# RWKV-7 attention followed by hash-routed experts: first expert's weights loaded during attention, the guard of w cut into 24 pieces among the experts, one outer fallback loop

## The chip, the cores and the metric

The kernel runs on one core of one Trainium2 chip. Time is device time in microseconds (us) of one execution; the median of several executions is given where there are several. A core has five engines with instruction streams of their own: TensorE (PE, with its weight loads as PEld), VectorE (DVE), ScalarE (ACT), GpSimd (POOL) and SyncE (SP, which only issues DMAs here). Each engine works its list in order, and engines wait for each other through semaphores. Transfers are moved by 16 DMA engines, which all queues share.

## The reference

The first part is a linear attention with a state per batch and head (4 batches, 8 heads, 768 steps, head size 40), the second a layer of 8 experts, in which a hash of the token's number chooses the expert.

```python
for t in range(S):
    y[:, :, t] = np.einsum('bhd,bhde->bhe', rt, state)
    Sa = np.einsum('bhde,bhe->bhd', state, at)
    state_decay = state * wt[:, :, None, :] - np.einsum('bhd,bhe->bhde', Sa, bt)
    state = state_decay + np.einsum('bhd,bhe->bhde', vt, kt)
...
expert_idx = token_ids * np.int64(2654435761) % np.int64(E)
for e in range(E):
    xe = x[expert_idx == e]
    out[expert_idx == e] = np.maximum(xe @ w1[e], 0.0) @ w2[e]
```

x is y with the heads side by side: 3072 rows of 320. w1 is 320 by 1024 and w2 1024 by 320 for each expert, all in float32, so each expert has two tensors of 1.31 MB.

## The kernel before

**Attention.** The sequence is cut into 12 chunks of 64 steps. A tile is one chunk of two batches with all heads, 24 tiles in all. The steps of a tile are spread over "ticks": `at_tick(tick, step)` puts a function into a list, which is sorted by tick and then executed once to write the instructions, so the order on each engine is written out by hand, over all tiles. The last tiles stand at ticks 30 and 31. The products of the decays w are formed in six rounds in the tiles `pb` and `qb` (L267 and L268), two buffers of each in the pool `work`. `paced` (L221) makes a DMA wait for the last TensorE instruction written so far, so that a load is not issued long before its tick. Loads of r, v, a, b and k go through SyncE's queue, one to two ticks ahead. Step "y" of a tile (L737) computes its rows of x, `xs`, and stores them with two DMAs from GpSimd's queue to `x_rows` in device memory (L753). At the end of attention its pools are closed, and their memory is used again.

**Routing.** In the ticks from 8 on, small steps sort the tokens: `src_all` and `idx_all` hold the rows of each expert in groups of 128, three groups of an expert and one group for the rests of four experts.

**Experts.** From here the order on an engine is chosen by the tile framework's scheduler, which follows the order of the program, priorities and buffers. `gather` (L938) fetches 128 rows of x with an indirect DMA from GpSimd (`xg`, six buffers), duplicates the last 64 columns on ScalarE, transposes three blocks on TensorE and copies them to `xt` on VectorE. `up` (L949) multiplies with w1 in two halves of four blocks; the blocks are evicted in turn by ScalarE and VectorE into `ht`, and five PSUM banks carry them. `down` (L979) multiplies with w2, and `put` (L969) copies the result on ScalarE and stores it with an indirect DMA. `load_w1` and `load_w2` load an expert's weights from SyncE's queue into two and six buffers; the first loads stand right behind the end of attention (L921, L927, L994).

**The guard and the fallbacks.** The decays are clamped to the range LO to HI for attention. After the experts all of w is read once more in six pieces of 128 by 1280 (L1018 to L1024), on VectorE: clamped, compared with itself, and the differences counted into `wbad`. From the count come four small numbers (L1026 to L1037). If any w was out of range, a slow loop over the sequence computes x anew (L1052), and a second loop (L1098) repeats the experts; the second loop also handles experts with more tokens than there are slots. With these inputs both loops run zero times, but each engine has to load the counts and pass both loops.

Of the kernel before, what the change touches and what calls it, by code (L numbers as in the profile page):

```python
# [8 lines left out]
F32 = mybir.dt.float32  # L9
# [9 lines left out]
def kernel(  # L19
# [18 lines left out]
    P = 128  # L38
# [42 lines left out]
    WP = 6  # L81
    wbad = route.tile([P, WP], F32)


    def load_w1(e, name):
        t = wpool.tile([P, 2 * F + F // 2], F32, tag="w1", name=name)
        nc.sync.dma_start(t[:, 0:2 * F].rearrange("p (c f) -> p c f", c=2), e[0:2 * P].rearrange("(c p) f -> p c f", p=P))
        for x in range(2):
            nc.sync.dma_start(t[x * C:(x + 1) * C, 2 * F:].rearrange("p (f i) -> p f i", i=P),
                              e[2 * P:DM].rearrange("p (f x i) -> p x f i", x=2, i=P)[:, x])  # L90
        return t


    a_ctx = ExitStack()
# [162 lines left out]
    def decays(ri, t_load, t_clamp, t_chain, t_own, t_ex, t_ends, t_pair, t_recip, t_en, t_spread, t_turn):  # L257
# [5 lines left out]
        for i in range(4 * RN):  # L263
            @at_tick(t_load + (0.06 * i if ri > 2 else 0))
            def _(i=i):
                if i == 0:
                    x["pb"] = work.tile([P, HC * D], F32, tag="pb", name="pb")  # L267
                    x["qb"] = work.tile([P, (HC + 1) * D], F32, tag="qb", name="qb")  # L268
# [385 lines left out]
    def tile_b(u, t0):  # L654
# [83 lines left out]
        def _():  # L738
# [12 lines left out]
            for be in range(2):  # L751
                r0 = batch(g, be) * S + n * C
                nc.gpsimd.dma_start(x_rows[r0:r0 + C, :], xs[half(be)])  # L753
# [159 lines left out]

    ET = mybir.EngineType
# [6 lines left out]
    w1s[0] = load_w1(moe_w1[0], "w1_0")  # L921
# [5 lines left out]
    w1s[1] = load_w1(moe_w1[1], "w1_1")  # L927
# [5 lines left out]
    def load_w2(e, name):  # L933
        t = w2pool.tile([P, FP, DM], F32, tag="w2", name=name, bufs=6)
        nc.sync.dma_start(t[:], e.rearrange("(c p) d -> p c d", p=P))
        return t

    def gather(xt, j, idx):  # L938

        xg = mwork.tile([P, DM + C], F32, tag="xg", bufs=6, name="xg")  # L940
        nc.gpsimd.indirect_dma_start(out=xg[:, 0:DM], out_offset=None, in_=x_rows[:],  # L941
# [5 lines left out]
        nc.vector.tensor_copy(xt[:, :, j * P:(j + 1) * P], p[:])  # L947

    def up(xt, w1, ht, n):  # L949
        def part(f):  # L950
            return slice((f % 2) * C, (f % 2 + 1) * C)
        for f0 in range(0, FP, 4):
            banks = []
            for f in range(f0, f0 + 4):
                banks.append(bank([P, n], "up_ps", "up", 5))
                rows = part(f)
                w = 2 * F + (f // 2) * P
                nc.tensor.matmul(banks[-1][:], lhsT=w1[rows, w:w + P], rhs=xt[rows, 2, 0:n], start=True, stop=False)  # L958
            for f in range(f0, f0 + 4):
                p = banks[f - f0]  # L960
                for c in range(2):
                    nc.tensor.matmul(p[:], lhsT=w1[:, c * F + f * P:c * F + (f + 1) * P], rhs=xt[:, c, 0:n],  # L962
# [16 lines left out]
    def down(ht, w2, j, idx, apart):  # L979
        p = bank([P, DM], "dn_ps")  # L980
        for f in range(FP):
            nc.tensor.matmul(p[:], lhsT=ht[:, f, j * P:(j + 1) * P], rhs=w2[:, f, :],  # L982
# [3 lines left out]
    def down_shared(hts, w2q, idx):  # L986
        p = bank([P, DM], "dq_ps")
        for f in range(FP):
            for q in range(4):
                nc.tensor.matmul(p[q * QTR:(q + 1) * QTR, :], lhsT=hts[q][:, f, FULL:SLOTS], rhs=w2q[q][:, f, :],  # L990
# [156 lines left out]
```

## Time and profile before

| | us |
|---|---|
| median of 3 runs | 741.28 (730.99 to 743.15) |
| profiled execution | 735.78 |
| its span, first to last instruction | 734.0 |
| attention, to its last matmul | 450.9 |
| seam: from there to the first `up` matmul | 20.4 |
| experts: from there to the last `down` matmul | 251 |
| from there to the end of the span | 11.5 |

The profile is of one execution. Rows of the timeline give start, duration, engine, line of the kernel, operation, output and inputs, how many of them, and in brackets how long the engine had been idle and what ended that. In the chain of waits a row is start, duration and what the end of the program waited for at that time. "issue" is time in which no wait shows. Windows give for each engine the busy microseconds and the number of instructions, then the clock that was granted to TensorE as a share of full speed, the busy share of the DMA engines and GB/s.

### The profile page before, as it was taken

What the parts mean: (1) busy time and instruction counts of PE and PEld (TensorE: products, weight loads), DVE (VectorE), ACT (ScalarE), POOL (GpSimd) and SP (SyncE); (2) the same over time, 40 slices, a digit from 0 to 9 for tenths busy, and PEclk for the clock granted to TensorE, in tenths of its full rate; (3) what the DMA queues carried; (4) which work ended last, traced back from release to release, by engine and by line L of the source; (5) the groups of instructions that cost most, each with busy time, mean ns of one, the idle gap of its engine ahead of it and who ended that gap; (6) DMA issues with size and microseconds to landing.
All of it is one profiled execution on the core that took longest, in us unless ns stands there. A gap on an engine that the chain in (4) does not pass through costs nothing.

```text
span 734.0 us, 23938 instructions
## 1 busy us (share of the span) xinstructions
PE 613.1 (84%) x10398; PEld 462.2 (63%) x10398; DVE 339.3 (46%) x704; ACT 309.4 (42%) x688; POOL 272.9 (37%) x343
## 2 busy tenths in 40 slices
PE   0436689789978998998998994598999999999993
PEld 0335568668867887887887884254656565565652
DVE  6789968835864684576397212116320110111100
ACT  2475656655775576786855561111110101101110
POOL 1786556443646483465241111503123030210111
PEclk9987679966997698899999998599999999999998
DMA  8565134523463453465244324977413342120000
GB/s 156 112 114 115 23 63 87 117 55 66 95 110 65 74 97 53 84 112 92 39 57 58 71 58 142 351 242 245 145 34 119 115 157 95 44 90 9 27 3 29
DMA packets 156748, 70.15 MB, mean 96 GB/s; under 512 B 134942, under 2 KB 149791, under 8 KB 156640
## 3 DMA queue, kind: packets, MB, share of 16 engines
q1 hardware_dynamic: 146336, 51.53, 31.1%
q0 software_dynamic: 5952, 16.08, 8.8%
q8 instruction: 82, 1.34, 0.7%
q10 hardware_dynamic: 4352, 0.98, 0.7%
q14 instruction: 26, 0.21, 0.1%
HBM read 56.73 MB, written 12.16 MB: 94 GB/s over the span
## 4 chain that ended last, share of the span: by engine, by line
PE 53%; issue 18%; DVE 11%; DMA 6%; POOL 5%; ACT 5%; SPq 1%; POOLq 0%; DVEq 0%; ACTq 0%
PE dn_ps L982 7%; PE up_ps L962 6%; PE r_ps L219 5%; PE y_ps L219 5%; PE s_ps L219 4%; PE rc_ps L219 4%; PE u_ps L219 3%; PE a_ps L219 3%; PE z_ps L529 2%; PE sd_ps L762 2%; POOL xg L941 2%; PE t_ps L534 2%; PE c_ps L219 2%; DMA z_all<-in_k_dram 2%; DVE ub L568 2%
## 5 line engine op out<-in xcount | busy, mean ns | idle before, releaser
L982 PE MATMUL dn_ps<-w,ht 128*128 128x320 f32 x384 | 104.9, 433 | 0.0
L972 POOL DMA_INDIRECT out_dram<-o,idx_all x26 | 25.7, 987 | 190.0 <-ACT o L971 182.8
L962 PE MATMUL up_ps<-xt,w 128*128 128x416 f32 x256 | 93.9, 520 | 0.0
L982 PEld LDWEIGHTS dn_ps<-w,ht 128*128 128x128 f32 x384 | 72.8, 190 | 32.1 <-issue 1.9
L753 POOL DMA_DIRECT2D x_rows<-xs x48 | 26.3, 553 | 149.4 <-DVE xs L750 103.3
L962 PEld LDWEIGHTS up_ps<-xt,w 128*128 128x128 f32 x256 | 47.5, 191 | 45.8 <-issue 45.8
L568 DVE TENSOR_TENSOR ub<-ub,outer 128x31 f32<-128x31 f32 (+15 forms) x186 | 65.0, 349 | 6.4
L565 DVE TENSOR_TENSOR outer<-ub,nb 128x31 f32<-128x31 f32 (+15 forms) x186 | 62.6, 337 | 4.6
L965 DVE TENSOR_SCALAR ht<-up_ps 128x416 f32<-128x416 f32 x32 | 18.9, 591 | 94.8 <-PE up_ps L962 94.8
L947 DVE COPY xt<-xg_ps 128x384 f32<-128x384 f32 x24 | 12.1, 551 | 101.8 <-PE xg_ps L946 101.8
L971 ACT COPY o<-dn_ps 128x320 f32<-128x320 f32 x24 | 10.2, 425 | 101.6 <-PE dn_ps L982 101.6
L703 DVE TENSOR_TENSOR mr<-rc_ps,after 128x1024 f32<-128x1024 f32 x24 | 29.3, 1221 | 50.4 <-PE rc_ps L219 50.4
L529 PE MATMUL z_ps<-ident,z_all 128*128 128x128 f32 x192 | 32.7, 325 | 15.1 <-DVE z_all L460 12.5
L967 ACT ACTIVATE ht<-up_ps 128x416 f32<-128x416 f32 x32 | 15.9, 514 | 63.8 <-PE up_ps L962 63.8
L460 POOL TENSOR_TENSOR z_all<-z_all,qt 128x320 f32<-128x320 f32 x40 | 34.2, 864 | 14.2 <-DMA z_all<-in_k_dram 12.5
L219 PE MATMUL rc_ps<-rt,cv 64*64 64x64 f32 x1536 | 37.5, 243 | 1.9 <-ACT cv L686 1.1
L941 POOL DMA_INDIRECT xg<-x_rows,src_all x26 | 27.2, 1045 | 28.7 <-PE xg_ps L946 15.7
L529 PEld LDWEIGHTS z_ps<-ident,z_all 128*128 128x128 f32 x192 | 26.3, 168 | 17.8 <-DVE z_all L460 12.8
L958 PE MATMUL up_ps<-xt,w 64*128 64x416 f32 x128 | 30.1, 562 | 7.8 <-DVE xt L947 3.2
L351 ACT COPY qt<-qt 64x320 f32<-64x320 f32 (+1 forms) x63 | 31.2, 495 | 12.0 <-DVE qt L326 8.2
L219 PEld LDWEIGHTS rc_ps<-rt,cv 64*64 64x64 f32 x1536 | 30.6, 151 | 8.6 <-issue 5.3
L714 ACT COPY x_all<-nc_ps 64x512 f32<-64x512 f32 x44 | 25.5, 580 | 24.3 <-PE nc_ps L712 23.8
(186 smaller groups left out, 1214.7 us busy)
## 6 DMA issues: line engine op xcount, KB each, us to landing
w<-in_moe_w_dram SPq DMA_DIRECT2D x8, 1280.0 KB, 17.5
w<-in_moe_w_dram SPq DMA_DIRECT2D x8, 1024.0 KB
r<-in_r_dram SPq DMA_DIRECT2D x48, 80.0 KB, 3.3
x_all<-in_v_dram SPq DMA_DIRECT2D x48, 80.0 KB, 3.7
py<-p_rows POOLq DMA_DIRECT2D x24, 160.0 KB
x_rows<-xs POOLq DMA_DIRECT2D x48, 80.0 KB
wt<-in_w_dram SPq DMA_DIRECT2D x6, 640.0 KB, 3.9
z_all<-in_b_dram SPq DMA_DIRECT2D x46, 80.0 KB, 3.3
```

Source lines behind the costliest of these rows:

```text
L219: pe_last[0] = nc.tensor.matmul(out_, lhsT=lhsT, rhs=rhs, start=start, stop=stop, skip_group_check=True).ins
L351: nc.scalar.copy(qt[d[0], d[1], cols], qt[src[0], src[1], cols])
L460: eng.tensor_tensor(t, t, by.rearrange("p (h e) -> p h e", e=D), op=OP.mult)
L529: pe_last[0] = nc.tensor.transpose(dst, src, ident[:]).ins
L565: nc.vector.tensor_tensor(tv, ub[:, 0:j + 1, j:j + 1].to_broadcast([P, j + 1, m]), nb[:, j, j + 1:].unsqueeze(1).to_broadcast([P, j + 1, m ...
L568: nc.vector.tensor_tensor(o, o, tv, op=OP.add)
L703: nc.vector.tensor_tensor(t[:].rearrange("p two h t -> p (two h) t"), p[:].rearrange("p two (h t) -> p (two h) t", t=C), after[:].unsqueez ...
L753: nc.gpsimd.dma_start(x_rows[r0:r0 + C, :], xs[half(be)])
L941: nc.gpsimd.indirect_dma_start(out=xg[:, 0:DM], out_offset=None, in_=x_rows[:], in_offset=bass.IndirectOffsetOnAxis(ap=idx, axis=0))
L958: nc.tensor.matmul(banks[-1][:], lhsT=w1[rows, w:w + P], rhs=xt[rows, 2, 0:n], start=True, stop=False)
L962: nc.tensor.matmul(p[:], lhsT=w1[:, c * F + f * P:c * F + (f + 1) * P], rhs=xt[:, c, 0:n], start=False, stop=(c == 1))
L982: nc.tensor.matmul(p[:], lhsT=ht[:, f, j * P:(j + 1) * P], rhs=w2[:, f, :], start=(f == 0), stop=(f == FP - 1))
```

## The change

- Expert 0's weights are no longer loaded after attention. `first_weights` takes buffers of `pb` and `qb`, which are now in a pool `carry` that stays open, and loads w1 into the two of `pb` and w2 into the two of `qb`, in 12 DMAs at ticks 20.5, 21.1 and so on to 27.1, each paced. `up` and `down` now take a function that gives the slice of a weight.
- The last chunk's stores of x go through SyncE's queue.
- Expert 1's weights are loaded after the first expert's fourth gather has landed (`hold_back`). Gathers have five buffers instead of six, w2 five instead of six.
- The guard is cut into 24 pieces of 128 by 320. `look` issues four loads at the end of each of the experts 0 to 5, `judge` takes four in each of the experts 1 to 6, with four buffers; `verdict` stands ahead of the last expert's `down`s. The scheduler then places them: on SyncE's queue four pieces come first behind attention, a fifth, then the weights of expert 1 (w1, w2), of expert 2, w2 of expert 3, three pieces, w2 of expert 4, four pieces, w2 of expert 5, and the other pieces. On VectorE four pieces and a fifth are judged among expert 0's copies to `xt`, seven ahead of expert 1's copies to `xt`, seven behind these and ahead of expert 1's first eviction, and the last five between its evictions.
- Both fallback loops stand inside one loop that runs once if either is needed, and zero times otherwise; a fourth count tells which.

```diff
-    WP = 6
+    WP = 24
...
+    def hold_back(dma):
+        if held:
+            tc.add_manual_dep(dma.ins, held[-1].name,
+                              mybir.DependencyInfo(mybir.DependencyClass.Sync, mybir.DependencyReason.SCHED_ONLY))
...
-                    x["pb"] = work.tile([P, HC * D], F32, tag="pb", name="pb")
-                    x["qb"] = work.tile([P, (HC + 1) * D], F32, tag="qb", name="qb")
+                    x["pb"] = carry.tile([P, HC * D], F32, tag="pb", name="pb")
+                    x["qb"] = carry.tile([P, (HC + 1) * D], F32, tag="qb", name="qb")
...
-                nc.gpsimd.dma_start(x_rows[r0:r0 + C, :], xs[half(be)])
+                (nc.sync if last else nc.gpsimd).dma_start(x_rows[r0:r0 + C, :], xs[half(be)])
...
+    def first_weights():
+        w1, w2 = moe_w1[0], moe_w2[0]
+        h = HC * D
+        a = [carry.tile([P, h], F32, tag="pb", name=f"w1_0{i}") for i in range(2)]
+        b = [carry.tile([P, (HC + 1) * D], F32, tag="qb", name=f"w2_0{i}") for i in range(2)]
...
+        for i in range(2):
+            for j in range(2):
+                cols = slice(j * F // 2, (j + 1) * F // 2)
+                yield nc.sync.dma_start(a[i][:, cols], w1[i * P:(i + 1) * P, cols])
+            for x in range(2):
+                yield nc.sync.dma_start(a[i][x * C:(x + 1) * C, F:].rearrange("p (f i) -> p f i", i=P),
+                                        w1[2 * P:DM].rearrange("p (f x i) -> p x f i", x=2, i=P)[:, x, 2 * i:2 * i + 2])
+        for i in range(2):
+            for j in range(2):
+                c0 = 4 * i + 2 * j
+                yield nc.sync.dma_start(b[i][:, 2 * j * DM:2 * (j + 1) * DM].rearrange("p (c d) -> p c d", d=DM),
+                                        w2[c0 * P:(c0 + 2) * P].rearrange("(c p) d -> p c d", p=P))
+
+    weights = first_weights()
+    for i in range(12):
+        at_tick(NU - 3.5 + 0.6 * i, order=7)(lambda: paced(next(weights)))
...
+    def look(n):
+        for i in range(len(seen), len(seen) + n):
+            wt = mwork.tile([P, m], F32, tag="wt", name="wt", bufs=n)
+            nc.sync.dma_start(wt[:], wq[:, i * m:(i + 1) * m])
+            seen.append(wt)
+
+    def judge(n):
+        for i in range(len(seen) - n, len(seen)):
+            wt = seen[i]
+            wc = mwork.tile([P, m], F32, tag="wc", name="wc", bufs=1)
+            nc.vector.tensor_scalar(wc[:], wt[:], LO, HI, op0=OP.max, op1=OP.min)
+            nc.vector.scalar_tensor_tensor(wt[:], wc[:], 0.0, wt[:], op0=OP.add, op1=OP.not_equal, accum_out=wbad[:, i:i + 1])
...
+        nc.vector.tensor_scalar(ctl[:, 3:4], ovin[0:1, E - 1:E], 0.0, None, op0=OP.is_gt)
+        nc.vector.tensor_tensor(ctl[:, 3:4], ctl[:, 3:4], bad[:], op=OP.max)
...
+        if e == 0:
+            held.append(g)
+            w1s[1] = load_w1(moe_w1[1], "w1_1")
+            w2s[1] = load_w2(moe_w2[1], "w2_1")
+            held.pop()
...
         if q == 3:
+            if e == E - 1:
+                bad, ctl = verdict()
             down_shared([hts[e - 3 + i] for i in range(4)], [w2s[e - 3 + i] for i in range(4)],
                         idx_all[:, NMT + e // 4:NMT + e // 4 + 1])
+        if 0 < e < E - 1:
+            judge(per)
         for j in range(TPE):
             down(ht, w2s[e], j, idx_all[:, e * TPE + j:e * TPE + j + 1], True)
...
+            look(per)
...
+    some = nc.values_load(ctl_i[0:1, 3:4], min_val=0, max_val=1)
+    with tc.For_i(0, some, 1):
+        nblk = nc.values_load(ctl_i[0:1, 0:1], min_val=0, max_val=S // STEP)
+        with tc.For_i(0, nblk, 1) as i:
```

## The prediction

> **What bounds the kernel now.** I read the page first: busy shares, then the 40 slices.
>
> ```profile
> PE 613.1 (84%) x10398; PEld 462.2 (63%) x10398; DVE 339.3 (46%) x704; ACT 309.4 (42%) x688; POOL 272.9 (37%) x343
> PE   0436689789978998998998994598999999999993
> PEclk9987679966997698899999998599999999999998
> GB/s 156 112 114 115 23 63 87 117 55 66 95 110 65 74 97 53 84 112 92 39 57 58 71 58 142 351 242 245 145 34 119 115 157 95 44 90 9 27 3 29
> ```
>
> TensorE has the work; a slice is 18.35 us. Behind the start-up it is full except at slices 24 and 25 (440 to 477 us), the seam between attention and experts, where the DMA engines suddenly move 351 GB/s, and in the last slice. So the edits are worth what these places and the guard of w cost. Next, the chain of waits in order of time over the seam (start, us, what):
>
> ```profile
> 450.95 0.50 DVE xs L750
> 451.73 0.53 POOL x_rows L753
> 452.26 5.53 DMA x_rows<-xs
> 457.79 0.02 issue
> ...
> 459.63 1.01 POOL xg L941
> 460.65 0.30 issue
> 460.95 0.97 POOL xg L941
> ```
>
> The last rows of x leave at 451.7, land at 457.79 (5.5 us after issue), GpSimd works off its semaphores for 1.84 us, and only then starts the gathers, 1.26 us apart. The timeline of the same stretch gives the end of the seam, and later the first two `up`s:
>
> ```profile
> 469.51 0.87 PE L946 MATMUL xg_ps<-ident,xg 128*128 128x128 f32 x3 [0.37 <-DMA xg<-x_rows,src_all]
> 471.30 3.15 PE L958 MATMUL up_ps<-xt,w 64*128 64x416 f32 x8 [0.91 <-DVE xt L1005]
> ...
> 503.53 1.49 DVE L1024 SCALAR_TENSOR_TENSOR wt<-wc,wt 128x1280 f32<-128x1280 f32 x1
> 503.94 2.08 POOL L941 DMA_INDIRECT xg<-x_rows,src_all  x1 [0.30 <-issue]
> ...
> 511.84 0.24 ACT L943 COPY xg<-xg 128x64 f32<-128x64 f32 x1 [2.19 <-DMA xg<-x_rows,src_all]
> 511.99 0.92 ACT L967 ACTIVATE ht<-up_ps 128x416 f32<-128x416 f32 x2
> 512.56 1.66 PE L958 MATMUL up_ps<-xt,w 64*128 64x416 f32 x6 [1.56 <-ACT ht L967]
> ```
>
> From the last matmul of attention (ends 450.93) to the first of expert 0's `up` are 20.4 us. Expert 1's `up` takes 17.19 us (502.65 to 519.84); in the chain, expert 6's takes 14.83 (660.48 to 675.31): 2.36 lost. ScalarE is in order, and its evictions stood behind copies of gathers that came late. The last view is the tail, by windows of 2 us:
>
> ```profile
> 723.29 0.97 POOL L972 DMA_INDIRECT out_dram<-o,idx_all  x1 [3.34 <-DVE it L1095]
> 724.00:726.00 2.00, 0.00 (x0) 0.00 (x0) 0.00 (x0) 0.00 (x0) 0.26 (x1) 1.00 0.28 94
> 726.00:728.00 2.00, 0.00 (x0) 0.00 (x0) 0.00 (x0) 0.00 (x0) 0.00 (x0) 0.86 0.00 0
> ```
>
> The result has landed by 726; the other 8.0 us of the span (734.0) hold no work, only two loops passed over and the end.
>
> **The change, part by part. (1) Seam.** Expert 0's 2.6 MB are loaded during attention, expert 1's wait behind the fourth gather, the last two pairs of x stores move from GpSimd's to SyncE's queue. Step by step, with the times of before:
> - xs is ready at 451.45. Two stores on SP: the nearest row is `p_rows<-pt`, an SP store of twice the size: 0.48 us on the queue, 2.1/3.0/5.3 us to landing (min, median, max). The second lands at 451.45 + 0.5 + 3.0 = 455.0, against 457.79; bounds 454.1 and 457.3.
> - GpSimd's wait list is as long as before: 1.84, so the gathers start at 456.85.
> - The fourth gather's instruction ends 3 x 1.26 + 0.95 later, at 461.6. With the weights in flight it took 5.1 us more until its transpose (464.41 to 469.51); a quiet gather (at 537.40) took 2.07 to ScalarE's copy. Now in flight: four or five pieces of w, 0.16 MB each. I take 2.1: 463.7.
> - New beside it: five pairs of guard instructions on VectorE, among the `xt` copies. [...]The row: beside the guard, gathers took 2.08 and 1.93 us, elsewhere 0.95. [...]by the row 2.1 for two. The first piece of w comes only near 459.3 (19 waits on SP, then 3.3 to landing), when two gathers are through; I take 1.0. A guard half ahead of `xt`: 0.3.
> - From transpose to `up`: 1.79 as before. Start 466.8 instead of 471.30: **4.5 us won** (bounds 0 and 6.8).
> The clock stays cold: it fell to half by 455, some 4 us after the last matmul, and rose in the 474 us window, 3.3 us after `up` began; ten idle microseconds are still too many. Neither gain nor loss.
>
> **(2) The twelve early loads.** 2.62 MB at the 356 GB/s of the saturated stretch are 7.4 us of DMA in some 65; on SP twelve issues of 0.4 to 0.6 us, behind which the loads of r, v, a, b, k queue. These have cover: issued 1 to 1.8 ticks of 11.1 us early, they need 3.1 to 4.7. 0 (bounds -0.5 and +3; a microsecond per microsecond late if the cover is gone).
>
> **(3) The guard.** Six pairs of 1280 columns (0.83 + 1.49 + 0.08) become 24 of 320: between 0.6 (proportional) and 1.26 each (two times the 0.59 of the 416-column eviction); I take 0.85, 20 us of VectorE instead of 14. The order on VectorE decides: seven pairs stand ahead of the `xt` copies of expert 1, seven more ahead of its first eviction, and each waits for its piece of w, which queues on SP behind weights. Up to the seventh piece the queue holds six weight tensors of 1.31 MB, seven pieces and the gathers of expert 1 (0.8): 9.8 MB, 27.6 us at 356 GB/s from 464.7, so 492.3, judged by 493.2; the copies are due at 501.11 - 4.5 = 496.6. 3.4 us spare. The next seven, with four buffers and 3.3 us a round trip, end at about 505, when the fifth bank is due at 506: no stall. But VectorE is at it while GpSimd issues the gathers that ScalarE waits for, as before. Of the 2.36 us I let 1.4 stand: **1.0 won** (bounds -3 and 2.4).
>
> **(4) Tail.** The verdict moves ahead of the last `down`s (0.2 us of TensorE either way). One loop end with its all-engine waits is passed instead of two, one load of a register instead of three. Half of 8.0 is 4; I keep one for the closing: **3.0 won** (bounds 0 and 5).
>
> **(5) Fewer buffers.** Five for gathers instead of six: in the order of ScalarE and GpSimd each group of copies keeps its place and size, one gather later. 0 (bounds 0 and +2). Expert 0's other tiles: the same matmuls. 0.
>
> Sum: 4.5 + 1.0 + 3.0 = 8.5. The profiled execution took 735.78 (span 734.0 and 1.8 around it): 727.3. It was 5.5 under the median of the three runs, 741.28, which spread over 12 us; from that median the sum gives 732.8. I name the middle, 730.
>
> **Rivals.**
> *A, the forecast* (0.55): 727 to 733.
> *B, everything at its best* (0.25): stores land in 2.1 us, [...]the guard's stall goes, the loop end costs 5: 6.8 + 2.4 + 5 = 14.2, 721.6 from the profiled execution, 727.1 from the median. For it: the DMA engines are nearly idle between 451 and 464; against: the guard runs in just that stretch.
> *C, the seam hardly shortens* (0.14): if the late landing is not the weights' doing but GpSimd's own[...] the seam gives 1 and the rest 3: 732 to 737. Against: quiet gathers land in 2.1.
> *D, VectorE's order turns on TensorE* (0.06), the other side. The pieces of w stand behind 9.8 MB; if that stretch runs at the 245 GB/s of slice 27, it takes 40 us, the seventh piece is judged at 505.6, 9.0 us after the copies are due, and the second seven, round trip by round trip, add 3. Then 8.5 - 12 is a loss of 3.5: 745. It decides from 9.8 MB in 31 us (316 GB/s), and eats the whole gain at 248. Against: 340 to 365 GB/s as long as the queue was full.
>
> Two per cent (15 us) is about what a measurement of this kernel can tell from no change. B and the lucky end of A, measured against the median, make "faster" 0.31; D's worst 0.04; the rest 0.65. Range: 721 (B's low end) to 738 (C's high end, and a profiled-like spread above A).
>
> **What would show it.** Expert 0's first `up` matmul some 16 us after attention's last (20.4 before), x stores 3.0 us to landing, gathers landing 2 us after issue with one or two of 1.5 to 2 us length; no `w` load between 451 and 464; the `xt` copies of expert 1 straight after their transposes; expert 1's `up` at about 16.2 us; some 5 us from the landing of the last result to the end. Wrong if VectorE's guard rows show waits on `wt` with TensorE idle behind them, if an attention tick is longer than 11.1 us near 340 to 400, or if the tail keeps its 8 us.

## The result, and the profile after

The changed kernel takes 731.92 us (median of 20 runs, 723.80 to 742.22), the kernel before 740.79 (20 runs beside it, 730.99 to 746.29). The ratio is 0.9892 (95% interval 0.9859 to 0.9926): 8.9 us between the medians, a little over half of two per cent. The profiled execution took 730.9 us, its span is 729.1. Ratios with an interval leave runs out that a lower clock disturbed; medians are over all runs, and differ by up to 14 us from chip to chip for the same kernel.

The page of the changed kernel, busy shares and slices (18.2 us each):

```profile
PE 621.6 (85%) x10398; PEld 470.0 (64%) x10398; DVE 345.7 (47%) x759; ACT 310.0 (43%) x688; POOL 269.7 (37%) x339
...
PE   0345779889997998999999899399999999999995
PEclk9997679865998698699999999689999999999998
...
GB/s 137 116 116 132 2 77 91 103 66 71 82 120 70 70 79 77 62 108 123 68 81 99 91 59 58 144 344 320 140 44 91 76 214 97 55 91 18 27 4 29
```

The hole at the seam is now one slice (the 3), the 344 GB/s stand behind it, and the last slice is fuller. The chain of waits over the seam, start, us and what:

```profile
458.64 0.50 DVE xs L765
...
459.15 0.47 SPq L768
...
459.67 2.14 DMA x_rows<-xs
...
463.02 1.01 POOL xg L984
...
464.33 0.96 POOL xg L984
```

The last store lands 2.14 us after its issue (5.53 before), and the first gather follows 1.21 us after the landing (1.84 before). The timeline of the same kernel, for expert 0's last transposes, the begin of both first `up`s, the guard and the last result:

```profile
470.67 0.87 PE L989 MATMUL xg_ps<-ident,xg 128*128 128x128 f32 x3 [0.47 <-DMA xg<-x_rows,src_all]
472.95 3.14 PE L1000 MATMUL up_ps<-xt,w 64*128 64x416 f32 x8 [1.41 <-DVE xt L1085]
...
503.14 0.49 DVE L1052 SCALAR_TENSOR_TENSOR wt<-wc,wt 128x320 f32<-128x320 f32 x1
...
505.59 1.67 PE L1000 MATMUL up_ps<-xt,w 64*128 64x416 f32 x8 [0.84 <-DVE xt L990]
...
506.87 0.99 POOL L984 DMA_INDIRECT xg<-x_rows,src_all  x1 [0.30 <-issue]
...
512.97 1.72 PE L1000 MATMUL up_ps<-xt,w 64*128 64x416 f32 x8
...
722.31 0.97 POOL L1014 DMA_INDIRECT out_dram<-o,idx_all  x1 [3.33 <-ACT o L1013]
```

From xs to the first `up` matmul are 14.3 us (20.4 before). The gather beside the guard took 0.99 us, not the 2.08 of before. Expert 1's second half of `up` (512.97) follows the first without a wait. And the end, by windows:

```profile
724.00:726.00 2.00, 0.00 (x0) 0.00 (x0) 0.00 (x0) 0.00 (x0) 0.00 (x0) 0.71 0.16 53
726.00:728.00 2.00, 0.00 (x0) 0.00 (x0) 0.00 (x0) 0.00 (x0) 0.00 (x0) 0.50 0.00 0
```

The result has landed by 726 and the span ends at 729.1: 3.1 us without work, where there were 8.0.

One place got worse. In the timeline of attention, two ticks of the kernel before,

```profile
390.81 0.49 DVE L750 TENSOR_TENSOR xs<-y_ps,py 128x320 f32<-128x320 f32 x1 [0.63 <-PE y_ps L219]
...
392.51 0.18 DVE L892 TENSOR_SCALAR src_all<-idx_all 128x26 int32<-128x26 int32 x1 [0.67 <-DMA idx_all<-slot_tokens]
...
403.57 0.49 DVE L750 TENSOR_TENSOR xs<-y_ps,py 128x320 f32<-128x320 f32 x1 [1.56 <-PE y_ps L219]
```

and the same two after the change:

```profile
395.33 0.49 DVE L765 TENSOR_TENSOR xs<-y_ps,py 128x320 f32<-128x320 f32 x1 [0.86 <-PE y_ps L234]
...
400.07 0.18 DVE L907 TENSOR_SCALAR src_all<-idx_all 128x26 int32<-128x26 int32 x1 [3.70 <-DMA idx_all<-slot_tokens]
...
405.62 0.69 PE L234 MATMUL x_ps<-ut,no 32*32 32x32 f32 x32 [2.86 <-DVE ut L591]
...
411.28 0.49 DVE L765 TENSOR_TENSOR xs<-y_ps,py 128x320 f32<-128x320 f32 x1 [3.11 <-PE y_ps L234]
```

A step of the routing sits in VectorE's list and waits 3.70 us for the loads of the indices (0.67 before); what stands behind it, the next tick's `ut`, comes late to TensorE, which stood idle for 2.86 us (1.57 before). From xs to xs are 15.95 us instead of 12.76. Part of that is clock: it was granted at half from 407.41 to 410.82, right behind this gap.

From span to span (734.0 to 729.1, -4.9) the stages give: attention +7.7 (the start +0.7, ticks 1 to 18 +3.8, the two ticks around the index step +3.2, then nothing), seam -6.0, expert 0's `up` +1.3, expert 1's -2.5, expert 4's -1.7, the verdict's matmul among the experts +0.2, the end -3.9.

### The profile page after: what moved, and what is told of

Same layout as the page of the kernel before. It is cut to its first block, busy times and chain, and to the rows that moved or that the text cites. A ratio compares the mean times of both kernels' runs of the same rounds, so it can differ in the third digit from the quotient of the medians.

```text
span 729.1 us, 23958 instructions
## 1 busy us (share of the span) xinstructions
PE 621.6 (85%) x10398; PEld 470.0 (64%) x10398; DVE 345.7 (47%) x759; ACT 310.0 (43%) x688; POOL 269.7 (37%) x339
## 4 chain that ended last, share of the span: by engine, by line
PE 35%; issue 32%; DVE 12%; POOL 7%; DMA 7%; ACT 4%; SPq 2%; POOLq 0%; DVEq 0%; ACTq 0%
PE y_ps L234 5%; PE r_ps L234 5%; PE s_ps L234 4%; PE rc_ps L234 3%; PE u_ps L234 3%; POOL out_dram L1014 3%; DMA z_all<-in_k_dram 3%; POOL xg L984 3%; PE z_ps L544 2%; PE a_ps L234 2%; DVE ub L583 2%; DVE outer L580 2%; PE t_ps L549 2%; PE sd_ps L777 2%; PE c_ps L234 2%
## 5 line engine op out<-in xcount | busy, mean ns | idle before, releaser
L1014 POOL DMA_INDIRECT out_dram<-o,idx_all x26 | 25.8, 994 | 185.9 <-ACT o L1013 179.1
L768 POOL DMA_DIRECT2D x_rows<-xs x44 | 24.3, 555 | 139.4 <-DVE xs L765 93.0
L234 PE MATMUL rc_ps<-rt,cv 64*64 64x64 f32 x1536 | 39.5, 251 | 2.3 <-ACT cv L701 1.1
L544 PEld LDWEIGHTS z_ps<-ident,z_all 128*128 128x128 f32 x192 | 27.8, 175 | 20.6 <-DVE z_all L475 15.3
L234 PEld LDWEIGHTS rc_ps<-rt,cv 64*64 64x64 f32 x1536 | 32.2, 158 | 9.4 <-issue 6.2
L984 POOL DMA_INDIRECT xg<-x_rows,src_all x26 | 25.6, 984 | 32.1 <-PE xg_ps L989 17.2
L729 ACT COPY x_all<-nc_ps 64x512 f32<-64x512 f32 x44 | 25.6, 581 | 26.8 <-PE nc_ps L727 26.3
L765 DVE TENSOR_TENSOR xs<-y_ps,py 128x320 f32<-128x320 f32 x24 | 11.8, 490 | 50.4 <-PE y_ps L234 50.4
```

What stands on the lines that cost most here:

```text
L234: pe_last[0] = nc.tensor.matmul(out_, lhsT=lhsT, rhs=rhs, start=start, stop=stop, skip_group_check=True).ins
L544: pe_last[0] = nc.tensor.transpose(dst, src, ident[:]).ins
L729: nc.scalar.copy(x["x"][half(be), be], p[half(be)])
L984: g = nc.gpsimd.indirect_dma_start(out=xg[:, 0:DM], out_offset=None, in_=x_rows[:], in_offset=bass.IndirectOffsetOnAxis(ap=idx, axis=0))
L1014: st = nc.gpsimd.indirect_dma_start(out=out[:], out_offset=bass.IndirectOffsetOnAxis(ap=idx, axis=0), in_=o[:], in_offset=None, bounds_che ...
```

## The experiments

Twelve kernels ran, in four groups; those of a group share a chip and the runs of the kernel before. The times first:

| kernel | runs | median | before, median | ratio with 95% interval |
|---|---|---|---|---|
| a_idx_later | 12 | 741.43 | 746.50 | 0.9883 (0.982 to 0.9946) |
| a_two_loops | 20 | 740.56 | 746.50 | 0.9983 (0.9907 to 1.006) |
| a_stores_gpsimd | 4 | 739.79 | 746.50 | 0.9891 (0.9786 to 0.9997) |
| b_xg5 | 20 | 745.58 | 746.50 | 1.0002 (0.9965 to 1.004) |
| after_again | 22 | 744.44 | 753.34 | 0.9955 (0.9922 to 0.9987) |
| a_late_verdict | 22 | 743.87 | 753.34 | 0.9868 (0.9828 to 0.9908) |
| a_guard_spread | 6 | 740.54 | 753.34 | 0.9885 (0.9833 to 0.9937) |
| best1 | 20 | 742.93 | 753.34 | 0.9895 (0.9859 to 0.9931) |
| a_warm | 6 | 758.53 | 754.67 | none |
| best2 | 22 | 746.06 | 754.67 | 0.9947 (0.991 to 0.9984) |
| a_first_late | 22 | 744.00 | 754.67 | 0.9871 (0.9817 to 0.9924) |
| best3 | 6 | 733.31 | 745.13 | 0.9853 (0.9795 to 0.9912) |

The changed kernel itself gave 0.9892 on one chip and 0.9955 on another, with intervals that hardly touch, while its medians stand at 0.988 of the kernel before both times. So a ratio here is good to half a per cent at best, and most of what follows is read from the stages of the profiles, one execution each, in us:

| kernel | xs 18 to xs 20 | VectorE waits for indices | xs to `up` 0 | `up` 0 | `down` 0 to `up` 1 | `up` 1 | `up` 4 | last `down` to end |
|---|---|---|---|---|---|---|---|---|
| before | 23.9 | 0.67 | 20.35 | 16.36 | 14.99 | 17.19 | 16.34 | 11.5 |
| b_xg5 | 25.4 | 1.66 | 20.55 | 16.44 | 14.98 | 20.65 | 15.66 | 11.1 |
| after | 27.1 | 3.70 | 14.31 | 17.65 | 14.99 | 14.72 | 14.67 | 7.6 |
| after_again | 34.3 | 5.56 | 14.29 | 17.18 | 16.15 | 14.67 | 14.67 | 7.8 |
| a_idx_later | 30.3 | 0 | 14.36 | 16.93 | 15.36 | 15.50 | 14.67 | 7.7 |
| a_two_loops | 27.8 | 3.00 | 14.35 | 16.28 | 16.95 | 16.32 | 14.67 | 7.6 |
| a_stores_gpsimd | 28.6 | 3.77 | 14.79 | 16.19 | 16.81 | 16.31 | 15.63 | 8.4 |
| a_late_verdict | 26.8 | 2.13 | 14.23 | 16.87 | 15.36 | 15.03 | 14.67 | 7.7 |
| a_first_late | 29.7 | 2.18 | 14.06 | 16.98 | 16.43 | 14.67 | 14.67 | 7.6 |
| a_guard_spread | 33.0 | 3.89 | 14.24 | 17.47 | 14.99 | 14.67 | 14.67 | 7.6 |
| best1 | 23.9 | 0 | 14.22 | 17.10 | 14.99 | 14.67 | 14.67 | 7.8 |
| a_warm | 31.6 | 4.02 | 20.22 | 15.36 | 23.56 | 16.30 | 14.67 | 7.7 |
| best2 | 24.6 | 0 | 20.22 | 14.67 | 14.99 | 14.67 | 14.67 | 7.8 |
| best3 | 25.7 | 0 | 13.33 | 14.67 | 14.99 | 14.67 | 14.67 | 7.6 |

An `up` is counted to the first matmul of its `down`, "`down` 0 to `up` 1" from first matmul to first matmul; 14.67 and 14.99 are these stages without any wait. xs 18 and 20 are the 18th and 20th xs rows; in the kernel before they stand at 390.81 and 414.70.

### The index step one tick later

```diff
+        yield
+        yield
         nc.vector.tensor_scalar(src_all[:], idx_all[:], float(N - 1), None, op0=OP.min)
...
-    for i in range(14 + TPP):
+    for i in range(16 + TPP):
```

> The changed kernel with one edit: the step that turns the slot indices into gather indices (src_all) comes one tick later in VectorE's order. In the changed kernel VectorE waited 3.70 us in this step for the index loads (0.67 before), because early weight loads stand ahead of them on SyncE and in the DMA engines. Theory 1: this wait was on the path; it goes, attention's last matmul comes some 3.2 us earlier, the time falls from 731.9 to about 728.7. Theory 2: the wait was covered (TensorE then waits for something else that is as late, a load of r or v behind the weights): the step no longer waits, but attention ends where it did and the time stays within 1 us of 731.9.

The wait is gone, but in this profile the two ticks took 30.3 us, with the clock granted at half from 415.49 to 429.14. In the three later kernels that hold the same edit they took 23.9, 24.6 and 25.7, as in the old order (23.9 and 25.4); the seven profiles with the step in its place and the early loads show 26.8 to 34.3. Most of that is the clock. In a_guard_spread VectorE waited 3.89 us here. The windows of TensorE alone (us, busy, clock, DMA share, GB/s):

```profile
407.96:411.37 3.41, 3.41 (x76) 1.00 0.76 159
411.37:414.79 3.42, 0.62 (x17) 1.00 0.59 137
414.79:418.20 3.41, 3.41 (x75) 0.50 0.03 8
...
428.44:431.86 3.42, 3.42 (x50) 0.50 0.44 72
431.86:435.27 3.41, 3.41 (x92) 1.00 0.14 24
```

TensorE lacks work for one stretch of 3.4 us, and behind it works for five such stretches at half clock. By estimate half of these 17.07 us is lost: 8.5 of the 9.0 us by which the two ticks are longer than in the kernel before. A gap of 1.57 us stands at this place in every kernel, before the change too; the wait for the indices makes it 1.65 to 5.07. Behind the gap of 1.57 the clock fell in three of six profiles (b_xg5, this one and best3), behind the longer ones in all eight. With half of the time at half clock taken off, the two ticks take 23.4 to 25.8 us in the seven profiles with early loads and the wait, and 23.4 to 24.5 in the six in which VectorE waited for 1.66 us or less. So by estimate the wait itself costs 0.9 us on average, and the clock behind it 1.7 to 8.5 (0 to 6.8 in the six).

In the time the gain can't be seen: the median is 0.993 of before, the ratio 0.988. Theory 1 holds for the ticks of three kernels out of four; for the time it is neither shown nor refuted, and this profile, long by the clock, can't decide it.

### The loops one after the other

```diff
-    some = nc.values_load(ctl_i[0:1, 3:4], min_val=0, max_val=1)
-    with tc.For_i(0, some, 1):
-        nblk = nc.values_load(ctl_i[0:1, 0:1], min_val=0, max_val=S // STEP)
-        with tc.For_i(0, nblk, 1) as i:
+    nblk = nc.values_load(ctl_i[0:1, 0:1], min_val=0, max_val=S // STEP)
+    with tc.For_i(0, nblk, 1) as i:
```

and both loops one level out.

> The changed kernel with the fallback loops one after the other again, as before, and everything else of the change kept, the early verdict too. Theory 1: the shorter end is the one loop's doing: from the end of the last result store's instruction to the end of the span 9.7 us again instead of 5.8, and 3.9 us more time, about 735.8. Theory 2: it is the early verdict that shortened the end: the end stays near 6.8 us and the time within 1 us of 731.9.

Theory 1 falls. The last result store starts at 733.94, its instruction ends at 734.91, and the span ends 5.4 us later (5.8 in the changed kernel, 9.7 before). From the last `down` to the end are 7.6 us, as with one loop. (One of the 20 runs took 1357.58 us; why is not known.) This profile brought something else, in the timeline at expert 1:

```profile
504.90 0.33 DVE L1051 TENSOR_SCALAR wc<-wt 128x320 f32<-128x320 f32 x1 [5.91 <-DMA wt<-in_w_dram]
...
510.15 0.33 DVE L1051 TENSOR_SCALAR wc<-wt 128x320 f32<-128x320 f32 x1 [2.59 <-DMA wt<-in_w_dram]
...
513.63 1.47 DVE L990 COPY xt<-xg_ps 128x384 f32<-128x384 f32 x3
...
515.16 2.33 PE L1000 MATMUL up_ps<-xt,w 64*128 64x416 f32 x8 [2.81 <-DVE xt L990]
```

The transposes were done by 512.4, but the copies stood behind the seventh guard piece, whose data came late: TensorE idle for 2.81 us, where the wait without the guard is 0.84. Behind it the clock was granted at half from 516.04 to 519.45, and `up` took 16.32 us instead of 14.67. So it was in a_stores_gpsimd (16.31) and a_warm (16.30), too: the 16.3 of these three is the clock, not a stall of its own.

### The last stores on GpSimd's queue

```diff
-                (nc.sync if last else nc.gpsimd).dma_start(x_rows[r0:r0 + C, :], xs[half(be)])
+                nc.gpsimd.dma_start(x_rows[r0:r0 + C, :], xs[half(be)])
```

> The changed kernel with the last stores of x on GpSimd's queue again. In the changed kernel the last store landed 2.7 us after xs was ready, before the change 6.3 us. Theory 1: the late landing was the doing of the weights in flight, not of the queue: landing at most 3.5 us after xs, first gather about 0.7 us later than in the changed kernel, and 0.5 to 1.5 us more time, 732.4 to 733.4. Theory 2: GpSimd's own path is slow: landing 5 to 6 us after xs, and some 3 us more, about 735.

The chain of waits of this kernel:

```profile
465.95 0.50 DVE xs L765
...
466.74 0.54 POOL x_rows L768
467.28 2.10 DMA x_rows<-xs
```

It lands 2.10 us after issue on the queue that took 5.53 in the kernel before: the late landing was the doing of the weights in flight. GpSimd then needs 1.84 us to its first gather, as before. The queue is worth 0.5 us of the seam (14.79 to 14.3); theory 1. Its end is 0.8 us longer, too (8.4 to 7.6), which was not expected and is not explained.

### The kernel before with five buffers for gathers

```diff
-        xg = mwork.tile([P, DM + C], F32, tag="xg", bufs=6, name="xg")
+        xg = mwork.tile([P, DM + C], F32, tag="xg", bufs=5, name="xg")
```

> The kernel before with five buffers for gathers instead of six, nothing else. Expert 4's up took 16.34 us before and 14.67 after the change, which was not foreseen. Theory 1: the smaller number of buffers, which changes the order of gathers and result stores on GpSimd, took that stall away: expert 4's up 14.7 us, expert 1's up still about 17.2, 1.7 us less than before, about 739.1. Theory 2: the stall had another cause (the guard of w, or chance of one execution): expert 4's up 16.3 again or different by itself, and no change beyond 0.5 us that follows from the buffers.

Expert 4's `up` took 15.66 us, between the two theories, and the time is the same as before (1.0002). The order on GpSimd explains it. With six buffers a result store stands between this `up` and the three gathers that ScalarE has to copy, and they begin 2.8 us into it. With five the store comes ahead of `up`, and they begin 2.1 us into it here and in a_stores_gpsimd (15.63), 0.6 us into it in the other eleven kernels with five (14.67). In these two GpSimd pauses for 1.84 us first, and these two are the ones with the last x stores on its queue; why it pauses is not shown.

Expert 1's `up` took 20.65 us here instead of 17.19. That is not the buffers: behind a stall like the one before (1.92 us, 1.56 before) the clock was granted at half for 6.83 us, and half of that is the difference.

### The changed kernel again

> The changed kernel itself, as the measure for the other runs of this group and as a second profile of it. Both theories: 0.989 of the time before, within its interval. In the profile, the places at which one execution differs from another: if the seven guard pieces ahead of expert 1's copies are only just in time, the wait from expert 0's last down to expert 1's up is 1.9 us in one execution and up to 4 us in another, while up of experts 1 and 4 takes 14.7 to 16.4 us; if they have the 3.4 us to spare that were worked out, it is 1.9 us again.

The wait ahead of expert 1's `up` was 1.2 us longer here (16.15 against 14.99), 2.0 longer in a_two_loops and 1.8 in a_stores_gpsimd. The seventh guard piece is only just in time in one execution and late in others.

### The verdict late, with one loop

```diff
-            if e == E - 1:
-                bad, ctl = verdict()
...
+    bad, ctl = verdict()
     ctl_i = route.tile([1, 4], I32)
```

> The changed kernel with the verdict on w after the last down again, as before, and the one outer loop kept. With two loops and the early verdict the end took 5.4 us from the last result store, so the loops are not what was saved. Theory 1: the early verdict is: the end goes back to 9.5 us or so and the time is 3 to 4 us above the changed kernel. Theory 2: one loop and early verdict each save the same thing (either is enough): the end stays at about 5.8 us and the time within 1 us of the changed kernel.

In the timeline the verdict's last step comes after the last `down`, as it did before:

```profile
732.48 0.28 PE L1058 MATMUL bad_ps<-wsum,ones 128*128 128x1 f32 x2
...
733.28 0.16 DVE L1102 CAST ctl_i<-ctl 1x4 int32<-1x4 f32 x1
733.42 0.97 POOL L1014 DMA_INDIRECT out_dram<-o,idx_all  x1 [3.33 <-ACT o L1013]
```

and still the span ends 5.9 us after that store, 7.7 after the last `down`. Theory 2: either edit is enough for the whole 3.9 us. No kernel with everything else of the change but neither of the two was run, so another edit could have shortened the end in all of them. The rows of the loops' ends, where the engines wait for each other, speak against it. GpSimd's (how many; shortest, median and longest in ns; first and last start in us) are in the kernel before (L1052 the first loop, L1098 the second) and in a_two_loops (L1118 the first):

```profile
L1052 POOLq EVENT_SEMAPHORE  x12: 42/43/2214, 724.5 to 727.6; - x12
L1098 POOLq EVENT_SEMAPHORE  x13: 17/43/43, 728.7 to 730.7; - x13
...
L1118 POOLq EVENT_SEMAPHORE  x12: 42/43/43, 730.1 to 732.9; - x12
```

Before, the last store started at 723.29 and both loops' ends lie behind it, one after the other. In a_two_loops it started at 733.94: with the counts known early, the first loop's end is passed ahead of it, beside the last `down`. Here, as in the changed kernel, there is only one end to pass. In all three fast cases one loop's end is left behind the last store.

### The guard spread over the experts

```diff
-            nc.sync.dma_start(wt[:], wq[:, i * m:(i + 1) * m])
+            hold_back(nc.sync.dma_start(wt[:], wq[:, i * m:(i + 1) * m]))
...
-            look(per)
+            held.append(marks[-1])
+            look(per)
+            held.pop()
```

`marks` holds the 64-row matmuls of all `up`s. The scheduler, which pulled all 24 pieces ahead of expert 2, now leaves four to an expert.

> The changed kernel with the four guard pieces of an expert loaded only after the 64-row matmuls of its up, so that VectorE judges four per expert, none in the seam and none of seven ahead of expert 1's copies. Theory 1: the guard's place on VectorE costs 0.5 us in the seam and 0 to 3 us at experts 1 and 4: seam about 13.9 us, up of experts 1 to 7 at 14.7 us, wait before expert 1's up 1.9 us, 1 to 2.5 us less than the changed kernel. Theory 2: ScalarE's in-order copies of late gathers, not the guard, make the stalls of up: seam 0.5 us shorter at most, up of expert 1 still above 15.5 us, time within 1 us of the changed kernel.

In the timeline expert 1 runs without a stall:

```profile
519.98 1.67 PE L1002 MATMUL up_ps<-xt,w 64*128 64x416 f32 x8 [0.84 <-DVE xt L990]
521.58 5.85 PE L1006 MATMUL up_ps<-xt,w 128*128 128x416 f32 x16
...
527.36 1.67 PE L1002 MATMUL up_ps<-xt,w 64*128 64x416 f32 x8
```

and so it is in all four kernels with this edit. From the first matmul of `down` 0 to the end of `up` 1 they take 29.66 us, the seven other profiles with the guard of the change 29.7 to 33.3, on average 31.3 (a_warm apart), the kernel before 32.2. The seam hardly gains: 14.24. Theory 1 holds for the experts; its half microsecond in the seam is not there, and the six runs are too few to show it in the time.

### Three edits together

Indices later, guard spread, and expert 1's weights held to the fourth matmul of expert 0's `up`:

```diff
-        if e == 0:
-            held.append(g)
...
         up(xt, w1s[e], ht, SLOTS)
+        if e == 0:
+            held.append(marks[3])
+            w1s[1] = load_w1(moe_w1[1], "w1_1")
+            w2s[1] = load_w2(moe_w2[1], "w2_1")
+            held.pop()
```

> Three edits of the changed kernel together: the gather indices one tick later on VectorE, the guard spread over the experts, and expert 1's weights held back to the fourth matmul of expert 0's up instead of the fourth gather. Theory 1: up of expert 0 loses the 1.3 us that late gathers cost it (about 16.4 us), the guard gives 1 to 2.5 us and the index wait up to 3 us: 3 to 6 us less than the changed kernel, 0.992 to 0.996 of it. Theory 2: attention is held by the granted clock, and what a wait less gives is taken back by it: 1.5 to 3.5 us less, from the experts alone.

The late gathers do land sooner: ScalarE's last copy for expert 1 comes 17.4 us after xs instead of 21.5. But expert 0's `up` still takes 17.10. That reason falls, and the windows of TensorE alone show the right one (us, busy, clock, DMA share, GB/s). The kernel before, `up` from 471.30:

```profile
472.00:474.00 2.00, 2.00 (x8) 0.50 1.03 353
474.00:476.00 2.00, 2.00 (x6) 0.79 1.10 379
```

The changed kernel, `up` from 472.95:

```profile
476.00:478.00 2.00, 2.00 (x5) 0.50 0.97 250
478.00:480.00 2.00, 2.00 (x5) 0.73 1.06 357
```

TensorE is busy throughout, at half clock. From the share in the mixed window the clock rose at 474.84 and 479.08, 3.5 and 6.1 us after `up` began; half of that is what the `up` is longer than 14.67 (1.7 and 3.0). Over the eleven profiles without idle-time matmuls it was 3.2 to 6.1; the two with the stores and loads of before, 3.5 and 3.7, lie among the others. In all, the clock stood at half for 20.48 us before (from 454.37) and for 17.07 after (from 462.02). What decides when it comes back is not shown. The changed kernel's own two profiles gave 17.65 and 17.18 for this `up`, and of the nine profiles of the change and its variants two lie below the 16.36 and 16.44 of the old ones (16.19 and 16.28), seven above. That expert 0's `up` lost by chance and not by the change was the author's estimate; these values don't decide it.

The time, 0.986 by the medians, is 1.5 us under the changed kernel on that chip: the low end of theory 2, less than a comparison here can tell, and not the 3 to 6 us of theory 1; this one profile was 11 us shorter than after_again's.

### TensorE kept busy over the seam

```diff
+    def keep_warm(lhsT, n):
+        for _ in range(n):
+            nc.tensor.matmul(warm[:], lhsT=lhsT, rhs=first_w[0][:, 0:SLOTS], start=True, stop=True)
+
+    keep_warm(ident[:], 20)
...
+        keep_warm(xg[:, 0:P], n_warm)
```

> The changed kernel plus 26 matmuls whose result nobody uses (416 columns each), 20 between attention's last matmul and the first gathered transpose, one behind each gather's transposes and three behind the last. In all profiles so far TensorE's clock stands at half from about 4 us after attention's last matmul until 3.1 to 5.6 us after expert 0's up has begun, and that up takes 16.4 to 17.8 us where the others take 14.7. Theory 1: the clock stays at 1.00 if TensorE is not idle for long: transposes 0.4 us instead of 0.9, up of expert 0 14.7 us, 2 to 3.5 us less than the changed kernel (about 0.984 of before). Theory 2: the short matmuls between the gathers are not enough, the clock falls anyway, up of expert 0 keeps 16.4 or more: no change beyond 0.5 us, or a loss of as much by the matmuls in the way.

> The three edits of the version with indices later, guard spread and weights held back, and the 26 idle-time matmuls. Theory 1: all of them add up: seam about 14 us, up of expert 0 14.7 us, experts without stalls, attention without the index wait: 0.978 to 0.984 of the kernel before. Theory 2: only the clock of the seam counts on top of the changed kernel, the other three give under 1 us together: 0.984 to 0.987.

The clock stayed at 1.00 in every window of the seam, and in best2 expert 0's `up` took 14.67 us: theory 1 as to the clock. In the time neither kernel reached a theory's range (a_warm 1.005 by the medians, best2 0.9947), for the matmuls were twice as long as planned. The chain of waits of best2:

```profile
469.77 14.23 PE warm L980 x40
```

Each of the 20 matmuls stands as two in the trace (x40), 0.71 us together, and the first gather, ready after 7.9 us, waited for 14.2 us of them: `up` started 6 us late. a_warm lost more, by the guard. With the new instructions the scheduler put guard pieces ahead of expert 0's last two evictions on VectorE, and in its timeline

```profile
507.98 0.33 DVE L1061 TENSOR_SCALAR wc<-wt 128x320 f32<-128x320 f32 x1 [9.14 <-DMA wt<-in_w_dram]
...
510.29 1.34 PE L1034 MATMUL dn_ps<-w,ht 128*128 128x320 f32 x4 [1.32 <-DVE ht L1017]
...
514.83 11.70 PE L1034 MATMUL dn_ps<-w,ht 128*128 128x320 f32 x34 [3.19 <-DVE ht L1017]
```

VectorE waits for w, the evictions behind it wait with it, and TensorE stands still; behind the first wait the clock was at half for 6.83 us. Together with the seven pieces ahead of expert 1, the way from `down` 0 to `up` 1 took 23.56 us instead of 14.99. By the medians of six runs the kernel is slower than the one before; the ratio is not known.

### Expert 0's weights behind attention's loads

```diff
-        at_tick(NU - 3.5 + 0.6 * i, order=7)(lambda: paced(next(weights)))
+        at_tick(NU + 6 + 0.01 * i, order=7)(lambda: paced(next(weights)))
```

> The changed kernel with expert 0's twelve weight loads behind the last loads of attention instead of among its ticks. Theory 1: the early loads are what delays the index loads: VectorE's wait for them falls from 2.1 to 5.6 us (six profiles of kernels with early loads) to 0.7 to 1.7 us, and the two ticks around it take 24 to 25 us instead of 27 to 34; the weights are there by the seam or nearly so, and the seam stays within 2 us of the changed kernel's 14.4. Theory 2: the wait has another cause and stays above 2 us. For the time: if attention really pays 3 us or more for the early loads, this kernel is 2 us or more faster than the changed one; if the clock takes it back, it is equal or slower.

The 2.6 MB were issued from 455 to 463 and were there by the seam: xs to `up` is 14.06 us. So what shortens the seam is not that they come so early, but that no weights are in flight when the last rows of x are stored. The loads cost the last ticks 3.3 us instead (xs 20 to xs 24 took 39.5 us, in all other profiles 36.2 to 36.3). The index wait was 2.18 without them: above 0.67 and 1.66, at the low end of the kernels that have them. The two ticks took 29.7, of which 13.65 at half clock. Early loads are thus not shown to be the only cause of that wait; how much of it is theirs stays open. The time is that of the changed kernel within the intervals.

### All edits, with matmuls that fit

best2 with `keep_warm(ident[:], 10)` and one matmul behind each gather.

> The three edits (indices one tick later, guard spread, expert 1's weights held to the fourth matmul of expert 0's up) with 14 idle-time matmuls instead of 26: ten behind attention's last matmul and one behind each of the four gathers. The 20 took 14.2 us, 0.71 each, because each runs as two passes, and stood in the way of the gathered transposes for 5 us; ten take 7.1 us and end just as the first gather is ready, 7.8 us after xs. Theory 1: the clock stays at 1.00 with idle gaps of up to 1.1 us, transposes take 0.4 us, expert 0's up starts 13.6 us after xs and takes 14.7: by the changed kernel's 14.3 and 16.4 to 17.8 that is 2.4 to 3.8 us less, with the spread guard 4 to 7 us under the changed kernel, 0.979 to 0.983 of the one before. Theory 2: the clock falls in the gaps between the gathers: up of expert 0 16.4 us or more, 0.984 to 0.988 of before.

Its timeline:

```profile
458.88 7.25 PE L980 MATMUL warm<-w,ident 128*128 128x416 f32 x20 [0.59 <-DVE xs L765]
466.10 0.75 PE L1000 MATMUL xg_ps<-ident,xg 128*128 128x128 f32 x3
...
470.24 0.52 PE L1000 MATMUL xg_ps<-ident,xg 128*128 128x128 f32 x3 [0.63 <-DMA xg<-x_rows,src_all]
470.60 0.86 PE L980 MATMUL warm<-w,xg 128*128 128x416 f32 x2
471.67 1.67 PE L1014 MATMUL up_ps<-xt,w 64*128 64x416 f32 x8 [0.21 <-DVE xt L1094]
473.27 5.85 PE L1018 MATMUL up_ps<-xt,w 128*128 128x416 f32 x16
```

Its first 64-row group takes 1.67 us where it was 3.14, `up` starts 13.33 us after xs, and both stages together are 28.0 us against 32.0 in the changed kernel. From xs to the end of the span are 266.5 us (270.5 after, 283.1 before); the span, 724.8, is the shortest of all profiles. Against the kernel before the ratio is 0.9853 (0.9795 to 0.9912), the medians 733.31 and 745.13, with six runs. It is faster than the kernel before. The stages are those of theory 1; the ratio's middle lies in the range of theory 2, and its interval holds both. That the kernel is faster than the changed one (0.9892) is what the stages say and the times don't yet separate.

## Why the prediction was right

The sum was 8.5 us, the medians differ by 8.9, and 731.9 lies between the forecast's 730 and its 732.8 from the median. That they agree so well is luck in part: the terms did not all hold, and their misses cancel.

- **Seam: mechanism right, 6.0 instead of 4.5.** The store lands 2.7 us after xs is done (3.5 taken); GpSimd's waits 1.21 (1.84), since part of its list now runs while the stores are on their way on another queue (1.84 again in a_stores_gpsimd); the last gather's landing and what was put down for gathers beside the guard together 2.8 (3.1); transposes to `up` with the guard 2.3 (2.1). Of the cause a_stores_gpsimd is the proof. The microsecond put down for gathers beside the guard, the author's estimate, was too much: the four took 1.01, 0.96, 1.02 and 0.95 us. In the whole stretch one gather of nine took 1.27, beside a guard step of 320 columns (0.33 us); four others ran beside such a step, too, and took 0.94 to 1.02. The rows of 2.08 and 1.93 us were measured beside steps of 1280 columns (0.83 and 1.49 us).
- **Clock: "stays cold: neither gain nor loss" was half right.** It stays cold, but it rises between 3.2 and 6.1 us into `up`, and that moved expert 0's `up` by 1.3 us in the profiled execution. The prediction had taken one such value, 3.3 us (3.5 by the windows), for fixed.
- **The early loads: this is the step that failed.** "These have cover" was worked out for r, v, a, b and k; the five index loads, which stand on SyncE's queue among the same ticks, were not in the list, and a step in the middle of VectorE's list waits for them. It measured 3.2 us in the profiled execution, just outside the bound of 3, and in others the two ticks were up to 10 us longer. Nor does it cost "a microsecond per microsecond late": by the estimate at a_idx_later the wait itself costs about 1 us, and the half clock behind the gap that it leaves on TensorE 1.7 to 8.5. The sign that was named for it, a tick longer than 11.1 us near 340 to 400, is there. That the loads cause the wait is likely and not separated (a_first_late).
- **Guard: 1.0 was right on average and for a reason that was too kind.** The pairs take 0.90 us (0.85). In the profiled execution all of the stall went (2.5 us); over the seven profiles of the changed kernel and its variants with that guard, the way from `down` 0 to the end of `up` 1 is 0.9 us shorter than in the kernel before (35.6 us in b_xg5, the other profile of the old guard, 3.4 of them by the clock). But "3.4 us spare" ahead of expert 1's copies was 0.4 in the profiled execution, and in others up to 2.0 us were missing. Rival D, with its 0.06, named the right mechanism: it cost 2 us in such executions, 1.7 more where the clock fell behind the wait, and 8.6 in a_warm.
- **Tail: 3.0 against 3.9, the size nearly right and the cause half right.** One loop's end is passed behind the last store instead of two, as forecast, but the outer loop is not needed for it: with two loops and an early verdict the first end is passed beside the last `down`. The prediction counted both edits into one gain without asking which.
- **Five buffers: 0 was within its bounds, but the groups did not keep their place.** A result store moved ahead of expert 4's `up`, which lost its stall of 1.7 us: 0.7 by the buffers alone, the rest only in the kernels with the last stores on SyncE's queue. Nothing of it shows in the time.

So the seam, the end and the experts gave more than was put down, 12.6 us from xs to the end of the span, and the medians kept 8.9. The rest must lie ahead of xs, and fits the two slow ticks and their clock; since attention differs by 15 us between the two profiles of the changed kernel (458.6 and 473.9 to the last xs, on two chips), this is inferred from the difference and not shown. From xs on the profiled execution is close to rival B (12.6 of its 14.2); attention brought it back to A.

## What to carry to other kernels

When a load is put into a queue, list everything that is issued on that queue behind it, small loads too, and ask which in-order engine waits for it in the middle of other work: here VectorE waited 2.1 to 5.6 us for five loads of indices, 13 KB in all. A gap on TensorE can cost more than its own length (in a_guard_spread 17.07 us at half clock stood behind a stretch of 3.42 us with 0.62 us of work): look at the granted clock behind it before the stage is called bound by work. A scheduler that pulls filler work forward because its data has no dependency puts it ahead of work that others wait for; tie its load to the place where it belongs. And a gain that comes from two edits at once belongs to neither until each has been taken away alone.

## What was not expected of the hardware

- A store of 80 KB landed 2.14 us after issue on SyncE's queue (after, 71 GB/s in that stretch) and 2.10 on GpSimd's (a_stores_gpsimd), and took 5.53 on GpSimd's beside the weights (before, 225 to 363 GB/s).
- Four loads of 0.2 KB each held SyncE's queue for 4.7 us (a_first_late) to 7.2 us (after), nearly as long as the twelve loads of 2.6 MB when they were issued together (455 to 463 in a_first_late).
- In the profiles of before and after, from 200 us on, TensorE's granted clock stayed at each value for 3.41 us or a multiple of it, but for the last stretch, which the record's end cuts off. It fell 12 times, each time behind a stretch of 3.41 us in which TensorE was busy for at most 0.72 of it, and it fell behind each of the eight such stretches at full clock with less than half. It rose ten times, each time behind a stretch that was busy throughout. Around the index step it stayed at half for 3.41 us (after) to 17.07 us (a_guard_spread) with TensorE busy again; what decides that length is not shown.
- At the seam the clock came back 3.2 to 6.1 us after dense work began; with 14 idle-time matmuls (best3) it stayed at 1.00 in every window from 448 to 480, with gaps of up to 0.63 us on TensorE behind the first of them, and expert 0's `up` fell from between 16.2 and 17.7 us to 14.67.
- Two loops that ran zero times, behind a condition computed after the last `down`, left 11.5 us from there to the end (before), the same two with the condition known earlier 7.6 (a_two_loops), one with the condition late 7.7 (a_late_verdict): in these two only one loop's end lies behind the last store.
